# Gated linear attention followed by dropless mixture of experts: a new kernel with units across batches, transposed results by head pairs, routing beside the attention, and experts cut to their tokens

## The chip, the cores and the metric

One NeuronCore of one Trainium2 chip. The metric is the time of the kernel on the device in microseconds (us), median of several executions. All arithmetic is fp32, and each fp32 matrix product appears in the trace as two TensorE instructions.

## The reference

```python
# q, k, v, a_re, a_im: (B=4, H=8, S=768, D=48);  w1: (E=8, 384, 1024), w2: (8, 1024, 384)
mag = sqrt(a_re**2 + a_im**2);  z = (a_re + 1j*a_im) * minimum(mag, .999) / (mag + 1e-6)
for t in range(S):                       # per batch and head, state (D x D), complex
    state = z[t][:, None] * state + outer(k[t], v[t])
    y[t] = q[t] @ real(state)
x = y as (3072 tokens, H*D = 384)
logits = x @ w_gate;  e = argmax(logits);  gate_w = softmax(logits)[e]
out = gate_w * (relu(x @ w1[e]) @ w2[e])          # each token by its own expert
```

## The kernel before

The sequence is cut into chunks of 128 tokens, so there are 24 chunks, six to a batch. Two consecutive chunks of one batch form a unit (twelve units), and units follow one another batch by batch. A framework traces the program in the written order and sorts each engine's instructions itself when it builds; activations alone are held to the written order by `act` and `table`, since each change between the log/exp and the trigonometric tables is an `ACT_TABLE_LOAD` (line 135).

For a unit, `decay_steps` (lines 164 to 187) turns the gates into ln|z| and an angle on GpSimd, VectorE and ScalarE. `decay_sums` sums ln|z| over the tokens by a product with a triangular matrix (tile `csl`) and takes exp of the sum and of its negative (`E`, `Ei`). `decay_total` gets a chunk's whole decay from 16 small products with a column of ones (`ms`), whose moving operand has a single column. `angle_sums` (lines 231 to 236) sums the angles in the same way (`cst`), adds the last angle of the chunk before by a second product with `last`, and removes whole turns; `rotation` takes the sine and cosine.

`attention` (lines 283 to 315) is run per chunk. `product` (lines 251 and 255) multiplies q by `E` and k by `Ei` on GpSimd and the rotation onto both on VectorE, so a head has 96 columns. Then TensorE transposes each head of Q and K (`tp`), the transposes are copied out by ScalarE (`qt`) and VectorE (`kt`), `at` is K against Q, masked by `tri` into `am`, `dk` is K against v for the carried state `G`, and `y` is `am` against v plus `qt` against `G`. In `y` the stationary operand is `am` or `qt` (128 columns) and the moving one has the 48 columns of a head. The result is stored to `xd` in DRAM, transposed again (`tpx`, line 262) and multiplied by `w_gate` (`lp`, line 268). One `mm` helper (line 65) records all products.

Behind the attention stands a branch on the flag of gates out of range (line 370), then the routing in one piece (lines 451 to 564): argmax, gate, rank among the expert's tokens by prefix sums, and a product of one-hot matrices (`sp`) that puts the tokens into slots. Each expert has four tiles of 128 slots, whatever the number of its tokens; further tiles run under a branch at the end. For each expert `gather` (line 577) fetches its rows by indirect DMA, `turn` (line 590) transposes them to 512 columns, `expert` computes `hps` (24 products of 512 columns), then four tiles of `yps` (8 products of 384 columns each), scales by the gate and scatters the rows to the output (line 612). The weights are loaded two experts ahead (lines 106 and 108), the first two during the attention.

Of the kernel before, what the change touches and what calls it, by code (L numbers as in the profile page):

```python
# [22 lines left out]
L_MIN = -0.5  # the chunked form keeps exp(-128 * L_MIN) within fp32  # L23
# [10 lines left out]
def kernel(  # L34
# [19 lines left out]
    NT = N // P  # token tiles  # L54
    CB = S // P  # chunks of a batch
    U = 2  # chunks of a unit
    NU = NT // U
    W = U * DM
    CT = 4  # token tiles that each expert has in the static part
    NS = E * CT  # its slots, in tiles  # L60
    NR = (N - CT * P) // P  # no routing needs more tiles than that beyond them
    NB = NS + NR

# [3 lines left out]
    def copy(i, o, in_):  # L67
        (nc.scalar.copy if i % 2 else nc.vector.tensor_copy)(out=o, in_=in_)  # L68
# [4 lines left out]
    wp = ctx.enter_context(tc.tile_pool(name="wp", bufs=2))  # L73

    def const(shape, name, dt=FP):
        return cp.tile(shape, dt, name=name)

    ident = const([P, P], "ident")
    make_identity(nc, ident)
    tri = const([P, P], "tri")  # [s, t]: s <= t  # L80
    make_upper_triangular(nc, tri, val=1.0, diag=True)
    tri_turn = const([P, P], "tri_turn")
    nc.vector.tensor_scalar(out=tri_turn, in0=tri, scalar1=1.0 / math.pi, scalar2=None, op0=OP.mult)
    tri_x = const([P, P], "tri_x")  # s < t
    nc.vector.tensor_tensor(out=tri_x, in0=tri, in1=ident, op=OP.subtract)
    ones = const([P, P], "ones")
    nc.vector.memset(ones, 1.0)
    last = const([P, P], "last")  # [s, t]: s == 127
    nc.gpsimd.affine_select(
        out=last, in_=ones, compare_op=OP.is_ge, fill=0.0, base=1 - P, pattern=[[0, P]], channel_multiplier=1  # L90
    )
    mhalfpi = const([P, 1], "mhalfpi")
    nc.vector.memset(mhalfpi, -0.5 * math.pi)

    wg = const([P, KD, E], "wg")
    good = const([P, NU], "good")
    lg = const([P, NT, E], "lg")
    flag = const([1, 1], "flag", I32)

    xd = dr.tile([N, DM], FP, name="xd")  # the attention's result, by token  # L100

    W_T = {}

    def load_w(e):
        a = wp.tile([P, KD, F], FP, tag="w1", name="w1t")
        nc.sync.dma_start(out=a, in_=w1[e].rearrange("(i p) f -> p i f", p=P))
        b = wp.tile([P, KF, DM], FP, tag="w2", name="w2t")
        nc.sync.dma_start(out=b, in_=w2[e].rearrange("(i p) d -> p i d", p=P))
        W_T[e] = a, b

    # ---------------------------------------------------------------- attention
    log = ExitStack()
    xl = log.enter_context(tc.tile_pool(name="xl", bufs=2))
    psL = log.enter_context(tc.tile_pool(name="psL", bufs=1, space=PSUM))
    att = ExitStack()
    ld = att.enter_context(tc.tile_pool(name="ld", bufs=2))
    un = att.enter_context(tc.tile_pool(name="un", bufs=2))
    ch = att.enter_context(tc.tile_pool(name="ch", bufs=2))
    psM = att.enter_context(tc.tile_pool(name="psM", bufs=1, space=PSUM))
    psT = att.enter_context(tc.tile_pool(name="psT", bufs=3, space=PSUM))  # L120
    psA = att.enter_context(tc.tile_pool(name="psA", bufs=1, space=PSUM))
    psY = att.enter_context(tc.tile_pool(name="psY", bufs=1, space=PSUM))
    psD = att.enter_context(tc.tile_pool(name="psD", bufs=1, space=PSUM))
# [16 lines left out]
    def load(u, names):  # L140
        for nm, src in names:
            t = ld.tile([P, U, H, D], FP, tag=nm, name=nm)
            for c in range(U):
                b, s = divmod(u * U + c, CB)
                nc.sync.dma_start(out=t[:, c], in_=src[b, :, s * P : (s + 1) * P, :].rearrange("h t d -> t h d"))
            T[nm, u] = t.rearrange("p c h d -> p (c h d)")

    def load_a(u):
        load(u, (("ar", a_re), ("ai", a_im)))

    def load_qkv(u):
        load(u, (("q", q), ("k", k), ("v", v)))

    def decay_steps(u):
        """ln |z| and the half angle of z, z = a * min(|a|, .999) / (|a| + 1e-6)."""
        ar, ai = T["ar", u], T["ai", u]
        A = un.tile([P, W], FP, tag="A", name="A")
        L = un.tile([P, W], FP, tag="L", name="L")
        R = un.tile([P, W], FP, tag="R", name="R")
        LL = un.tile([P, U * H, 2, D], FP, tag="LL", name="LL")  # twice, for decay_total  # L160
        T["L", u], T["th", u] = LL, ai

        def s0():
            nc.gpsimd.tensor_tensor(out=A, in0=ar, in1=ar, op=OP.mult)
            nc.gpsimd.tensor_tensor(out=R, in0=ai, in1=ai, op=OP.mult)  # L165
            nc.vector.scalar_tensor_tensor(out=A, in0=A, scalar=2.0**-62, in1=R, op0=OP.max, op1=OP.add)
            act(out=L, in_=A, func=AF.Ln)

        def s1():
            act(out=R, in_=L, func=AF.Exp, scale=-0.5)  # L170
            nc.gpsimd.tensor_tensor(out=A, in0=A, in1=R, op=OP.mult)
            nc.vector.scalar_tensor_tensor(out=A, in0=ar, scalar=2.0**-62, in1=A, op0=OP.max, op1=OP.add)

        def s2():
            act(out=R, in_=R, func=AF.Ln, scale=1e-6, bias=1.0)
            nc.vector.tensor_scalar(out=L, in0=L, scalar1=0.5, scalar2=LN_CAP, op0=OP.mult, op1=OP.min)
            nc.vector.tensor_tensor(out=L, in0=L, in1=R, op=OP.subtract)

        def s3():
            act(out=A, in_=A, func=AF.Ln)  # L180

        def s4():
            act(out=A, in_=A, func=AF.Exp, scale=-1.0)
            nc.gpsimd.tensor_tensor(out=ai, in0=ai, in1=A, op=OP.mult)
            nc.vector.scalar_tensor_tensor(out=R, in0=L, scalar=-L_MIN, in1=ar, op0=OP.add, op1=OP.min)
            nc.vector.tensor_reduce(out=good[:, u : u + 1], in_=R, op=OP.min, axis=AX_X)
            nc.vector.tensor_scalar(  # L187
                out=LL, in0=bc(L.rearrange("p (x d) -> p x d", d=D), 2, 2), scalar1=L_MIN, scalar2=None, op0=OP.max
            )

        return [s0, s1, s2, s3, s4]

    def decay_angle(u):
        act(out=T["th", u], in_=T["th", u], func=AF.Arctan)

    def decay_sums(u, c):
        L = T["L", u]
        sl = slice(c * DM, (c + 1) * DM)
        if c == 0:
            T["E", u] = un.tile([P, W], FP, tag="E", name="E")  # L200
            T["Ei", u] = un.tile([P, W], FP, tag="Ei", name="Ei")
        cs = psM.tile([P, DM], FP, tag="mm", padded_shape=[P, 512], name="csl")
        mm(cs, tri, L[:, c * H : (c + 1) * H, 0])
        act(out=T["E", u][:, sl], in_=cs, func=AF.Exp)
        act(out=T["Ei", u][:, sl], in_=cs, func=AF.Exp, scale=-1.0)

    def decay_total(u):
        """exp of the chunks' sums of ln |z|, by [(re, im) d, head]."""
        ms = psM.tile([P, U, H], FP, tag="mm", padded_shape=[P, 32, 16], name="ms")
        L = T["L", u].rearrange("p x a d -> p x (a d)")  # L210
        for c in range(U):
            for h in range(H):
                mm(ms[0:DD, c, h : h + 1], L[:, c * H + h], ones[:, 0:1])
        M = un.tile([P, U, H], FP, tag="M", name="M")
        act(out=M[0:DD], in_=ms[0:DD], func=AF.Exp)
        T["M", u] = M

    def angle_sums(u, c):
        """The angle up to each token in turns, less the whole ones; on from the chunk before."""
        g = u * U + c  # L220
        if c == 0:
            T["fg", u] = un.tile([P, U * H, 2, D], FP, tag="fg", name="fg")
        hs = slice(c * H, (c + 1) * H)
        f = T["fg", u][:, hs, 1, :]
        first = g % CB == 0
        cs = psM.tile([P, H, D], FP, tag="mm", padded_shape=[P, 8, 64], name="cst")
# [452 lines left out]
```

## Time and profile before

| | |
|---|---|
| median of 3 runs | 862.42 us (859.28 to 866.72) |
| span of the profiled execution, first to last instruction | 852.1 us |
| median less that span | 10.3 us |
| TensorE busy in the span | 744.4 us (87%) |
| VectorE, GpSimd, ScalarE busy | 333.0, 224.4, 204.7 us |
| granted TensorE clock, mean over the span | 0.870 |

A busy TensorE isn't TensorE at its peak: products overlap, and the granted clock is either full (1.00, 2.4 GHz) or half (0.50, 1.2 GHz); a value between is a mean over a stretch that holds both.

### The profile page before, as it was taken

The page shows a single profiled execution, that of the slowest core. Times are in us where ns is not written, and L with a number is a line of the kernel's source. Part 1 is how long each engine was busy: PE and PEld are TensorE (multiplying, and loading weights), DVE is VectorE, ACT ScalarE, POOL GpSimd, SP SyncE. Part 2 cuts the span into 40 slices and gives each one's busy share as a digit, 9 for nine tenths or more (in the row PEclk, how much of TensorE's full clock was granted, in tenths as well). Part 3 has the DMA queues.
Part 4 walks back from the last instruction along what each step waited for, and adds up shares of the span by engine and source line. Part 5 has one row for each costly group of instructions (what it writes and reads, how often), then busy time and mean ns, then how long its engine had stood idle before and what let it go on. Part 6 is the DMA issues. An engine that isn't in the chain of part 4 may idle for free. (4 is left out here: it accounts for less than half of the span.)

```text
span 852.1 us, 8900 instructions
## 1 busy us (share of the span) xinstructions
PE 744.4 (87%) x3574; PEld 532.0 (62%) x3574; DVE 333.0 (39%) x499; ACT 204.7 (24%) x320; POOL 224.4 (26%) x177
## 2 busy tenths in 40 slices
PE   0589998999899898999991489999999999999995
PEld 0378886887878788888880435555555555555553
DVE  3577665655576376663426311111111111020200
ACT  4354244433444245533310000000000000000000
POOL 5551432616245053342000140202020303010101
PEclk9999777856897598986785679999999999999998
DMA  9475534323254232401000032324232323220000
GB/s 171 68 214 138 145 71 96 62 56 65 48 94 83 47 65 47 93 11 28 19 19 4 13 99 92 119 83 132 83 130 84 130 84 128 84 95 10 15 10 21
DMA packets 144322, 65.18 MB, mean 76 GB/s; under 512 B 127232, under 2 KB 138528, under 8 KB 144272
## 3 DMA queue, kind: packets, MB, share of 16 engines
q1 hardware_dynamic: 136720, 48.78, 25.0%
q0 software_dynamic: 4096, 11.02, 3.9%
q10 hardware_dynamic: 3456, 4.72, 1.5%
q8 instruction: 31, 0.51, 0.3%
q14 instruction: 19, 0.16, 0.1%
HBM read 55.06 MB, written 11.01 MB: 78 GB/s over the span
## 5 line engine op out<-in xcount | busy, mean ns | idle before, releaser
L65 PE MATMUL hps<-xt,w1t 128*128 128x512 f32 x384 | 168.0, 597 | 0.0
L65 PE MATMUL yps<-w2t,ht 128*128 128x384 f32 x512 | 166.4, 486 | 0.0
L65 PEld LDWEIGHTS yps<-w2t,ht 128*128 128x128 f32 x512 | 97.3, 190 | 69.5 <-issue 3.8
L65 PEld LDWEIGHTS hps<-xt,w1t 128*128 128x128 f32 x384 | 73.2, 192 | 89.1 <-issue 89.1
L612 POOL DMA_INDIRECT out_dram<-y,row x32 | 31.8, 995 | 285.1 <-DVE y L611 285.1
L611 DVE TENSOR_SCALAR y<-yps,gate 128x384 f32<-128x384 f32 x32 | 19.8, 618 | 165.4 <-PE yps L65 165.4
L65 PE MATMUL y<-v,am 128*128 128x48 f32 x384 | 75.5, 292 | 1.9 <-DVE am L291 1.8
L605 DVE TENSOR_SCALAR ht<-hps 128x512 f32<-128x512 f32 x32 | 22.1, 692 | 123.9 <-PE hps L65 123.9
L65 PEld LDWEIGHTS y<-v,am 128*128 128x128 f32 x384 | 65.2, 215 | 8.4 <-DVE am L291 3.2
L65 PE MATMUL y<-G,qt 96*128 96x48 f32 x320 | 69.5, 302 | 0.0
L65 PE MATMUL at<-qt,kt 96*128 96x128 f32 x384 | 65.2, 317 | 4.5 <-DVE am L291 4.3
L65 PEld LDWEIGHTS at<-qt,kt 96*128 96x128 f32 x384 | 58.8, 227 | 12.1 <-issue 8.1
L603 ACT ACTIVATE ht<-hps 128x512 f32<-128x512 f32 x32 | 19.1, 597 | 156.5 <-PE hps L65 133.9
L65 PEld LDWEIGHTS y<-G,qt 96*128 96x128 f32 x320 | 56.4, 220 | 0.0
L283 PE MATMUL tp<-ident,Q 128*96 128x128 f32 x192 | 41.0, 338 | 14.2 <-DVE Q L255 14.2
L251 POOL TENSOR_TENSOR Qe<-q,E 128x384 f32<-128x384 f32 x24 | 38.6, 1609 | 41.8 <-ACT E L129 40.0
L68 ACT COPY xt<-tp 128x512 f32<-128x512 f32 x8 | 4.7, 587 | 185.0 <-PE tp L590 185.0
L65 PE MATMUL csl<-LL,tri 128*128 128x384 f32 x48 | 26.1, 634 | 25.2 <-DVE LL L187 17.6
L165 POOL TENSOR_TENSOR R<-ai 128x768 f32<-128x768 f32 x12 | 18.1, 1512 | 109.6 <-DMA ai<-in_a_im_dram 109.6
L65 PE MATMUL ms<-ones,LL 128*96 128x1 f32 x384 | 42.0, 243 | 3.3 <-ACT Ei L129 3.3
L65 PEld LDWEIGHTS ms<-ones,LL 128*96 128x96 f32 x384 | 41.8, 196 | 4.4 <-ACT Ei L129 4.4
L283 PE MATMUL tp<-ident,K 128*96 128x128 f32 x192 | 41.6, 341 | 2.9 <-DVE K L255 2.9
(139 smaller groups left out, 987.8 us busy)
## 6 DMA issues: line engine op xcount, KB each, us to landing
w1t<-in_moe_w_dram SPq DMA_DIRECT2D x8, 1536.0 KB, 6.4
w2t<-in_moe_w_dram SPq DMA_DIRECT2D x8, 1536.0 KB
ar<-in_a_re_dram SPq DMA_DIRECT2D x24, 192.0 KB, 4.3
ai<-in_a_im_dram SPq DMA_DIRECT2D x24, 192.0 KB, 3.4
q<-in_q_dram SPq DMA_DIRECT2D x24, 192.0 KB, 3.8
k<-in_k_dram SPq DMA_DIRECT2D x24, 192.0 KB, 4.3
v<-in_v_dram SPq DMA_DIRECT2D x24, 192.0 KB, 3.9
xd<-x ACTq DMA_DIRECT2D x24, 192.0 KB, 1.9
```

What stands on the lines that cost most here:

```text
L65: return nc.tensor.matmul(o, lhsT=lhsT, rhs=rhs, start=start, stop=stop, skip_group_check=True)
L68: (nc.scalar.copy if i % 2 else nc.vector.tensor_copy)(out=o, in_=in_)
L165: nc.gpsimd.tensor_tensor(out=R, in0=ai, in1=ai, op=OP.mult)
L251: nc.gpsimd.tensor_tensor(out=e.rearrange("p h d -> p (h d)"), in0=T[src, u][:, sl], in1=T[dec, u][:, sl], op=OP.mult)
L283: nc.tensor.transpose(out=tp[0:DD, j], in_=X[:, hg * 4 + j], identity=ident)
L603: nc.scalar.activation(out=ht[:, f], in_=ps, func=AF.Relu)
L605: nc.vector.tensor_scalar(out=ht[:, f], in0=ps, scalar1=0.0, scalar2=None, op0=OP.max)
L611: nc.vector.tensor_scalar(out=y, in0=ps, scalar1=gates[i], scalar2=None, op0=OP.mult)
L612: nc.gpsimd.indirect_dma_start(out=out, out_offset=bass.IndirectOffsetOnAxis(ap=idx[i], axis=0), in_=y, in_offset=None, bounds_check=N - 1 ...
```

## The change

The kernel is written anew around the same mathematics.

- A unit is now one chunk position of all four batches (six units of four chunks), and it is handled in two halves of two batches. So four independent states are carried (`G0` to `G3`), and a chunk needs the one before it in its batch only four chunks later.
- The gate formula is shorter (three steps, `gate_steps`), with fixed bounds `A_MIN` and `T_MAX` in place of exact limits. Whether the gates lie within them is tested by `in_range` beside the experts. GpSimd's products move to VectorE; GpSimd keeps only DMAs.
- `ms` and the products with `last` are gone. The decay of a chunk is row 127 of `E`, stored to DRAM and read back by head dimension (`md`, `M`); the last angle goes through DRAM (`cd`) and is added to row 0 of the next unit's angles by an accumulating DMA.
- `results` computes the transposed result: v or `G` (48 columns) is stationary and `am` or `qt` (128 columns) moves. The two heads of a pair go to rows 0 and 64 of one PSUM tile `yt`. `finish` turns it back with one product per pair against `back`, which holds the identity and `w_gate` side by side, so that the logits come with it; `tpx` and `lp` are gone.
- All four `qt`/`kt` copies are ScalarE's.
- Routing runs in groups while the attention goes on (units 0 and 1, 2 and 3, 4), and only the last unit's share follows the attention. Experts are sorted by their number of tokens; place i has `CAPS[i]` columns. The expert of the first place is fixed, and its weights loaded, in the last unit.
- `hps` and the transposes have `CAPS[i]` columns; a last tile of at most 64 rows uses two or four column groups of TensorE, whose sums are added afterwards.
- Both fallbacks stand in one branch at the end.

```diff
+CAPS = (448, 416, 416, 408, 400, 384, 376, 360)
...
+        def s0():
+            act(out=A, in_=ar, func=AF.Relu, bias=a_low)
+            act(out=A, in_=A, func=AF.Ln, bias=a_min)
+            act(out=R, in_=A, func=AF.Exp, scale=-1.0)
+            tt(out=ai, in0=ai, in1=R, op=OP.mult)
+            ts(out=ai, in0=ai, scalar1=-T_MAX, scalar2=T_MAX, op0=OP.max, op1=OP.min)
+            act(out=R, in_=ai, func=AF.Square)
+        def s1():
+            act(out=R, in_=R, func=AF.Ln, bias=1.0)
+            stt(out=A, in0=R, scalar=0.5, in1=A, op0=OP.mult, op1=OP.add)
+        def s2():
+            act(out=R, in_=A, func=AF.Exp, scale=-1.0, bias=ln_eps)
+            stt(out=ar, in0=A, scalar=LN_CAP, in1=R, op0=OP.min, op1=OP.subtract)
...
+    def decay(u, half):
...
+        nc.sync.dma_start(out=md[g : g + HB, :].unsqueeze(0), in_=T["E", u, half][P - 1 : P])
+        for i in range(2):
+            nc.sync.dma_start(
+                out=M[i * D : (i + 1) * D, u, half * HB : (half + 1) * HB],
+                in_=md[g : g + HB, :].rearrange("o (h d) -> d o h", d=D),
             )
...
+    def angle(u, b0, b1):
+        th = flat(T["ai", u][:, b0:b1])
+        act(out=th, in_=th, func=AF.Arctan)
+        if u > 0:
+            nc.gpsimd.dma_start(
+                out=T["ai", u][0:1, b0:b1].rearrange("p b h d -> p (b h d)"),
+                in_=cd[1, u - 1 : u, b0 * DM : b1 * DM],
+                accum_op=OP.add,
             )
...
+    def results(u, b, hg):
+        half, c = divmod(b, HB)
+        V = T["v", u, half][:, c]
+        for hp in range(2 * hg, 2 * hg + 2):
+            o = [yt[i * 64 : i * 64 + D, hp] for i in range(2)]
+            for i in range(2):
+                mm(o[i], V[:, 2 * hp + i], T["am", u, b, hg][:, 2 * (hp % 2) + i], True, u == 0)
+            for i in range(2):
+                if u > 0:
+                    mm(o[i], T["G", b][0:DD, 2 * hp + i], T["qt", u, b, hg][0:DD, 2 * (hp % 2) + i], False, True)
...
+    def finish(u, b):
+
+        xb = psX.tile([P, HP, DD + E], FP, tag="xb", padded_shape=[P, 4, P], name="xb")
+        for hp in range(HP):
+            mm(xb[:, hp], T["ys", u, b][:, hp], back[:, hp])
...
+    for g in range(NT):
+        u, b = divmod(g, B)
...
+        at(results, g, 0)
+        at(state, g)
+        part(g, 0)
+        at(products, g + 2)
+        at(results, g, 1)
+        part(g, 1)
+        at(scores, g + 1, 0)
+        at(evict, g)
+        part(g, 2)
+        at(scores, g + 1, 1)
+        at(outer, g + 1)
+        part(g, 3)
+        at(finish, g)
...
+            if n > 64:
+                for f in range(KF):
+                    mm(ps[0:n], hs[:, f], wb[:, f], f == 0, f == KF - 1)
+                ts(out=y[0:n], in0=ps[0:n], scalar1=g, scalar2=None, op0=OP.mult)
+            else:
+
+                w = 32 if n <= 32 else 64
+                np_ = P // w
+                for f in range(KF):
+                    j = f % np_
+                    mm(ps[j * w : j * w + n], hs[:, f], wb[:, f], f < np_, f >= KF - np_)
...
+    for i in range(E):
+        turn(i)
+        if i + 1 < E:
+            gather(i + 1)
+        expert(i)
+        if i + 2 < E:
+            load_w(i + 2)
+        if i < NR_:
+            in_range(i)
```

`part` starts the gate work of the next unit at fixed quarters of a chunk. `in_range` loads a sixth of `a_re` and `a_im` (1536 columns each) and runs two VectorE operations over it.

## Rows read from the trace of the kernel before

**Rows 1.** Busy time of each engine, granted clock and DMA by stage (windows view).

```profile
0.00:47.12 47.12, 14.77 (x44) 8.38 (x45) 20.26 (x25) 19.42 (x24) 24.84 (x23) 1.00 0.88 128
47.12:447.83 400.71, 372.69 (x2484) 332.25 (x2484) 239.71 (x329) 159.78 (x255) 135.87 (x82) 0.79 0.32 72
447.83:496.65 48.82, 14.26 (x67) 11.87 (x67) 21.39 (x67) 2.23 (x3) 8.72 (x16) 0.57 0.11 30
496.65:842.39 345.74, 342.65 (x981) 179.51 (x980) 51.01 (x79) 23.22 (x39) 53.94 (x55) 0.99 0.25 83
842.39:852.10 9.71, 0.00 (x0) 0.00 (x0) 0.61 (x1) 0.00 (x0) 0.98 (x1) 0.64 0.02 5
```

Columns: stretch, its length, busy us of PE, PEld, DVE, ACT and POOL, granted clock, DMA share, GB/s.

**Rows 2.** Timeline of TensorE in the attention, at full clock (start, busy us, what).

```profile
86.60 0.88 PE L65 MATMUL csl<-LL,tri 128*128 128x384 f32 x2
87.32 0.60 PE L283 MATMUL tp<-ident,Q 128*96 128x128 f32 x4
...
89.40 0.39 PE L65 MATMUL y<-v,am 128*128 128x48 f32 x2
...
89.85 0.60 PE L283 MATMUL tp<-ident,K 128*96 128x128 f32 x4
90.29 1.48 PE L65 MATMUL dk<-v,K 128*96 128x48 f32 x16
91.60 0.51 PE L262 MATMUL tpx<-ident,x 128*128 128x128 f32 x3
91.95 1.06 PE L65 MATMUL at<-qt,kt 96*128 96x128 f32 x8
92.84 0.73 PE L65 MATMUL lp<-wg,xt 128*128 128x8 f32 x6
93.43 2.86 PE L65 MATMUL ms<-ones,LL 128*96 128x1 f32 x32
```

**Rows 3.** Windows of 2 us around two falls of the clock (columns as before).

```profile
98.00:100.00 2.00, 2.00 (x10) 1.70 (x9) 1.44 (x3) 0.00 (x0) 0.00 (x0) 0.50 0.64 86
...
146.00:148.00 2.00, 0.20 (x2) 0.14 (x2) 1.32 (x3) 1.98 (x4) 0.00 (x0) 1.00 1.15 269
...
150.00:152.00 2.00, 2.00 (x12) 1.94 (x11) 1.56 (x3) 0.61 (x2) 1.88 (x2) 0.50 0.03 5
```

**Rows 4.** Groups by line and shape: VectorE and ScalarE (busy us, mean ns).

```profile
L135 ACT ACT_TABLE_LOAD x26 | 33.4, 1283 | 1.2 <-PEq L665 0.8
L291 DVE TENSOR_TENSOR am<-at,tri 128x512 f32<-128x512 f32 x48 | 32.9, 686 | 21.6 <-PE at L65 21.5
...
L68 ACT COPY qt<-tp 96x512 f32<-96x512 f32 x48 | 27.7, 582 | 37.5 <-PE tp L283 37.2
...
L129 ACT ACTIVATE A<-A 128x768 f32<-128x768 f32 x24 | 20.3, 845 | 13.8 <-DVE A L172 13.6
...
L232 DVE TENSOR_TENSOR fg<-cst,r 128x384 f32<-128x384 f32 x24 | 13.2, 550 | 0.3
```

**Rows 5.** Timeline of TensorE in the start: its first product.

```profile
17.61 1.62 PE L65 MATMUL csl<-LL,tri 128*128 128x384 f32 x2 [17.61 <-DVE LL L187]
```

**Rows 6.** Timeline between attention and experts: end of the branch, token list.

```profile
453.77 0.14 POOL L451 IOTA eid<- 128x8 f32 x1 [54.77 <-SPq L370]
...
484.59 0.19 DVE L560 CAST tok<-sl 128x52 int32<-128x52 f32 x1
```

**Rows 7.** Timeline of TensorE over one expert.

```profile
541.70 20.77 PE L65 MATMUL hps<-xt,w1t 128*128 128x512 f32 x48
562.30 20.80 PE L65 MATMUL yps<-w2t,ht 128*128 128x384 f32 x64
582.94 1.04 PE L590 MATMUL tp<-ident,xg 128*128 128x128 f32 x8
```

**Rows 8.** DMA issues: engine, count, size, median us to landing.

```profile
w1t<-in_moe_w_dram SPq DMA_DIRECT2D x8, 1536.0 KB, 6.4
...
xd<-x ACTq DMA_DIRECT2D x24, 192.0 KB, 1.9
```

More of the change, by code (lines that the diff above doesn't have):

```diff
@@ L138, in table @@
         T["act"] = ins
[L140 to L161, printed above, removed]
-        def s0():
[L164 to L167, printed above, removed]
+    HB = B // 2
@@ new lines, with keys @@
+    owner = const([P, E], "owner", I32)
+    own0 = const([P, 1], "own0", I32)
+    tok = const([P, E, CT], "tok", I32)
+    row = const([P, E, CT], "row", I32)
+    gate = const([P, E, CT], "gate")
+    over = const([P, 1], "over")
+    head = const([P, E], "head")
+    caps = const([P, E], "caps")
+    for i, c in enumerate(CAPS):
+        nc.gpsimd.memset(caps[:, i : i + 1], float(c))
+    def keys(o):
+        cp_ = psD.tile([P, E], FP, tag="dk", padded_shape=[P, 512], name="cnt")
+        mm(cp_, ones, acc)
+        stt(out=o, in0=cp_, scalar=float(E), in1=rev, op0=OP.mult, op1=OP.add)
+        return cp_
@@ new lines, in gate_pieces, with p @@
+    def gate_pieces(n):
+        st = gate_steps(n, 0, B)
+        def p(f, *a):
+            return lambda: f(*a)
+        return {
+            -5: [p(table, "natural_log_exp_and_others"), st[0]],
+            -3: [st[1]],
+            -1: [st[2]],
+            1: [p(decay, n, 0)],
+            2: [p(decay, n, 1)],
+            3: [lambda: T["second"]() if n - 1 in GROUPS else None],
+            4: [p(table, "trig_and_small"), p(angle, n, 0, B)],
+            6: [p(turns, n, 0)],
+            7: [p(rotation, n, 0)],
+            9: [p(turns, n, 1)],
+            10: [p(rotation, n, 1)],
+        }
@@ L332 @@
+    GROUPS = {2: (0, 2), 4: (2, 4)}
+    load_gates(0, 0)
+    load_qkv(0, 0)
+    load_gates(0, 1)
+    load_qkv(0, 1)
+    for hp in range(HP):
+        for i in range(2):
+            nc.sync.dma_start(
+                out=back[i * 64 : i * 64 + D, hp, DD:], in_=w_gate[hp * DD + i * D : hp * DD + (i + 1) * D, :]
+            )
+    for half in range(2):
+        load_gates(1, half)
+    for half in range(2):
+        c0, c1 = half * HB, (half + 1) * HB
         table("natural_log_exp_and_others")
-        for f in steps:
+        for f in gate_steps(0, c0, c1):
@@ L355 @@
-    att.close()
-    bad = xl.tile([P, NU], FP, tag="bad", name="bad")
-    nc.vector.tensor_scalar(out=bad, in0=good, scalar1=0.0, scalar2=None, op0=OP.is_ge)
-    nc.vector.tensor_scalar(out=bad, in0=bad, scalar1=-1.0, scalar2=1.0, op0=OP.mult, op1=OP.add)
-    bp = psL.tile([1, NU], FP, tag="mm", padded_shape=[1, 512], name="bp")
+        angle(0, c0, c1)
+        turns(0, half)
+        rotation(0, half)
+    pieces = {1: gate_pieces(1)}
+    for i in sorted(pieces[1]):
+        if i < 0:
+            for f in pieces[1].pop(i):
+                f()
@@ new lines, in part, with at @@
+    def part(g, i):
+        for n in range(1, NU):
+            s = g * 4 + i - (n - 1) * B * 4
+            if s >= -5 and n not in pieces:
+                pieces[n] = gate_pieces(n)
+            if n in pieces:
+                for f in pieces[n].pop(s, []):
+                    f()
+    def at(f, g, *a):
+        if g < NT:
+            f(*divmod(g, B), *a)
+    at(products, 0)
+    at(products, 1)
+    at(scores, 0, 0)
+    at(scores, 0, 1)
+    at(outer, 0)
+    for g in range(NT):
+        u, b = divmod(g, B)
+        if b % HB == 0 and u + 1 < NU:
+            load_qkv(u + 1, b // HB)
+        if b in (1, 2) and u + 2 < NU:
+            load_gates(u + 2, b - 1)
+        if b == 0 and u in GROUPS:
+            T["second"] = route(*GROUPS[u])
+        if u == NU - 1 and b == 1:
+            T["second"] = route(NU - 2, NU - 1)
+            table("natural_log_exp_and_others")
+            T["second"]()
+            first_place()
+        at(results, g, 0)
[11 more added lines that the diff above has]
+        at(finish, g)
@@ new lines, with pool2, gather @@
+    T["second"] = route(NU - 1, NU)
+    places()
+    T["second"]()
+    gates_of_places()
+    att.close()
+    ex = ExitStack()
+    def pool2(name, bufs, **kw):
+        return ex.enter_context(tc.tile_pool(name=name, bufs=bufs, **kw))
+    wp = pool2("wp", 1)
+    xp = pool2("xp", 2)
+    hp = pool2("hp", 2)
+    yp = pool2("yp", 3)
+    rp = pool2("rp", 2)
+    psG = pool2("psG", 2, space=PSUM)
+    psH = pool2("psH", 4, space=PSUM)
+    psO = pool2("psO", 2, space=PSUM)
+    def gather(i):
+        xg = xp.tile([P, CT, DM], FP, tag="xg", name="xg")
+        for t in range(-(-CAPS[i] // P)):
+            n = min(P, CAPS[i] - t * P)
+            nc.gpsimd.indirect_dma_start(
+                out=xg[0:n, t],
+                out_offset=None,
+                in_=xd[:, :],
+                in_offset=bass.IndirectOffsetOnAxis(ap=tok[0:n, i, t : t + 1], axis=0),
+                bounds_check=N - 1,
+                oob_is_err=False,
+            )
+        T["xg", i] = xg
@@ new lines, in turn @@
+    def turn(i):
+        cap, xg = CAPS[i], T["xg", i]
+        xt = xp.tile([P, KD, CAPS[0]], FP, tag="xt", name="xt")
+        for d in range(KD):
+            tp = psG.tile([P, 512], FP, tag="tp", name="tp")
+            for t in range(-(-cap // P)):
+                n = min(P, cap - t * P)
+                nc.tensor.transpose(
+                    out=tp[:, t * P : t * P + n], in_=xg[0:n, t, d * P : (d + 1) * P], identity=ident[0:n, 0:n]
+                )
+            (nc.scalar.copy if d % 2 else nc.vector.tensor_copy)(out=xt[:, d, 0:cap], in_=tp[:, 0:cap])
+        T["xt", i] = xt
@@ L596, in expert @@
[L596 to L602 removed]
+                out=xg, out_offset=None, in_=xd[:, :], in_offset=bass.IndirectOffsetOnAxis(ap=ti, axis=0)
+            )
+            tp = psZ.tile([P, KD, P], FP, tag="mm", padded_shape=[P, 4, P], name="tpx")
```

870 lines of the change are left out of this document (497 added, 373 removed).

## The prediction

> **What bounds the kernel now.** I read the windows by stage first, since the page's mean over the span mixes four stages [rows 1]. Look there at TensorE's busy time against the length, and at the clock. The start (47.1 us) is bound by DMA and by the gate chain: TensorE has 14.8 us of work. In the attention (400.7 us) TensorE is busy 93%, VectorE 60%, ScalarE 40%, so TensorE sets the pace, but at a mean clock of 0.79. In the gap between attention and experts (48.8 us) nothing but routing runs. In the experts (345.7 us) TensorE is busy 99% at a clock of 0.99; only fewer columns can shorten that. The end (9.7 us) is the last scaling, scatter and drain.
>
> Next the timeline of TensorE, read by the starts of successive groups, since busy times overlap: 0.72 us for a `csl` pair, 0.112 each for `y` (0.45 for four), 0.11 for a transpose, 1.31 for 16 `dk`, 0.35 for three `tpx`, 0.111 each for `at`, 0.59 for six `lp`, 2.86 for 32 `ms` [rows 2]. `y` with 48 moving columns costs as much as `at` with 128: both have 128 stationary columns. Per chunk at full clock: 16 transposes 1.76, 16 `at` 1.78, `dk` 1.31 x 20/24 = 1.09, `y` 29.3 x 0.112 = 3.29, `tpx` 0.35, `lp` 0.59, `csl` 0.72, `cst` 0.72, `last` 0.60, `ms` 1.43; together 12.3 us. A chunk takes 400.7 / 24 = 16.7, a ratio of 0.74. The missing quarter is the clock and 7% idle time.
>
> Why the clock falls is seen in windows of 2 us. Of its 17 falls between 60 and 442 us ten come during or within 4 us of an `ms` burst, as the one to 0.50 at 98 us behind the burst of 93.43 [rows 2, 3]; most of the others follow a gap of TensorE, as that behind 146 to 148 us, where TensorE was busy 0.20 of 2 us [rows 3].
>
> **The start.** The first `csl` begins at 17.6 us [rows 5]; before, a whole second set of gates then shares the engines until the first chunk at 47.1 [rows 1]. Now half a unit goes through alone. From 17.6 I add the chain: `csl` pair at half clock 1.6, `E` and `Ei` 1.7, arctan and table 2.1, `cst` 1.6, five VectorE operations 2.7, two sines 1.7, products 1.5: about 30 us. The second half follows on the same ordered activations and unit 1's gates behind it, while chunks 0 and 1 last only some 25 us. I take 36; bounds 28 and 47.
>
> **TensorE in the attention.** `ms`, `last`, `tpx` and `lp` go: 2.97 us. Transposes, `at`, `dk`, `csl` and `cst` stay: 6.07. `results` has as many products as `y`, now with 48 stationary and 128 moving columns. No row shows that; the nearest is a transpose, 96 stationary and 128 moving at 0.11 [rows 2], so 29.3 x 0.111 = 3.26, nothing gained. `finish` adds eight products with 128 stationary and 104 moving columns, 0.89; routing's products about 0.2. Sum 10.4 us, against 12.3. The two heads of a pair write different rows of PSUM. Every row runs products one behind the other, so I take no overlap; an overlap in pairs would make `results` 1.6. The Trainium skill (TensorE: Matmul & The Clock Gate, Part 3) says that products in different column groups of the array run together; by that the sum would be 8.8 and the time that of the first rival. Against the change speaks the skill's TensorEngine Tiling (Array Packing), Key Properties: changing the tiling mode drains TensorE. No run here shows it. A group of four transposes is busy 0.60 us but starts its successor after 0.44 [rows 2], so an estimate is 0.16 lost per change, four changes a chunk, 16 us in all; by the rule 689 us, without it my sum.
>
> **VectorE and ScalarE.** Their work rises towards TensorE's. VectorE: 550 ns for 384 columns and 686 for 512 [rows 4] give 1.06 ns a column, so 0.96 for 768 and 1.77 for 1536. Per chunk: products 2 x 0.55 + 2 x 0.96 = 3.0 (half of it came from GpSimd), masks 1.37, states 0.8, turns 1.6, gates 4 x 1.77 / 4 = 1.8, small ones 0.3: 8.9. The routing of before took 21.4 us of VectorE for 24 chunks [rows 1], 0.9 per chunk: 9.8. ScalarE: 582 ns for 512 and 845 for 768 columns [rows 4], so 1.64 for 1536: copies and eviction 5 x 0.58, `x` 0.45, `E` and `Ei` 0.85, sines 0.85, seven gate functions 7 x 1.64 / 4 = 2.9, two table loads of 1.28 per unit 0.64: 8.6. So VectorE's 9.8 is the floor if TensorE got cheaper, and 10.4 TensorE's own.
>
> What waits behind what: the gate operations are now 1.6 to 1.8 us long, and a `qt` copy that comes behind one holds `at`; there are only two `tp` buffers and one `at`. `yt` is a single bank, so the results of a chunk wait for the eviction of the one before; `scores` of the next chunk stands between them in the written order and hides that. If it doesn't, each chunk pays the 0.58.
>
> **Time per chunk.** With the ratio of before, 0.74, 10.4 would become 14.1. `ms` stood before ten of seventeen falls, so I expect a clock nearer 0.88 than 0.79; TensorE's waits on the two fuller engines take back about 6%. Ratio 0.83: 12.5 us, 24 x 12.5 = 300 us. Bounds: 10.5 (no losses) and 15.5 (more waits than before), so 252 to 372.
>
> **Transfers.** `M` takes a store and two loads on SP's queue per half unit, the carry a store, a load, a VectorE operation, a store and a GpSimd accumulation. A store lands after 1.9 us, a weight load of 1.5 MB after 6.4 [rows 8]. None shows 4-byte pieces; bounds 2 and 6 each, I take 4 as for a short load, so a chain is 8 to 16 us. `M` is wanted about a unit later (50 us), the carry two thirds of a unit later: hidden, at nothing. Behind the waiting stores on SP's queue stand the q, k, v and gate loads and the stores of `x`; three buffers of halves cover them. The accumulation must land between `angle` and `turns`, some 6 us; if it's late, TensorE waits up to 5 us in each of five units, 25 us in all. The start moves 128 GB/s at a share of 0.88 [rows 1]; 28 MB in 300 us are 94 GB/s, about two thirds of that.
>
> **Gap.** The branch, 5.3 us up to 453.77, leaves this place [rows 6]; at the end one stands already. From there to the token list were 31 us [rows 6]. Now four chunks remain: one-hot matrices of 24 chunks (four operations, some 8 us) shrink to a sixth, 48 `sp` products (8.8) to eight, the tables of prefix sums go, the sorting by places comes. I count some 45 VectorE operations of 0.2 and four returns through TensorE: 14 us. From the list to the first `hps` stay 12.1 [rows 1, 6]. Together 26; bounds 18 and 36. The other groups of the routing now lie beside the attention and are in VectorE's 0.9.
>
> **Experts.** `hps` takes 20.60 us for 512 columns, four tiles of `yps` 20.64 (5.16 each) [rows 7]; an expert takes 345.74 / 8 = 43.2 [rows 1], so `turn` 1.96. The caps sum to 3208. `hps` 20.60 x 3208 / 512 = 129.1, `turn` 12.3. Tiles: 24 full ones 123.8, five short ones of 16 to 64 rows at 5.16 if nothing overlaps, 25.8; with full overlap 7.7. I take the first, as the rows run one after another: 291, bounds 273 and 295. The reference's inputs give 421 to 338 tokens per expert, all under their caps, and smallest `a_re` 0.85 above `A_MIN`, so the branch for other inputs isn't taken. `in_range` adds 12 VectorE operations of about 1.8 us, beside a VectorE busy 51 of 346 us, and 9.4 MB of loads beside 83 GB/s [rows 1]: nothing. Extra work of short tiles sits on ScalarE and VectorE too, and the last three places have none.
>
> **Sum.** 36 + 300 + 26 + 291 + 9.7 = 663 us of span instead of 852.1. The median stands 10.3 above the span of the profiled run, so 673. A measurement of this kernel can tell about 1% from no change.
>
> **Rivals.** First, the pairs overlap: TensorE's chunk 8.8, VectorE's 9.8 becomes the bound, some 11.3 us with waits, 271; experts 273. 36 + 271 + 26 + 273 + 20 = 626. For it: different PSUM rows; against: no row has two products at once. Second, the queues jam: copies and masks behind long gate operations, 15.5 us a chunk, 745. For it: three engines between 8.6 and 10.4; against: GpSimd no longer sits in the chain. Third, the experts wait: weights of place i+2 and the `in_range` loads can start only when expert i frees its buffers, 2 x 6.4 us for weights [rows 8] and some 6.6 for the check; if VectorE's check stands ahead of the next expert's copies, up to 13 us of these 19 are left in each of five places, 65 in all: 738. For it: one SP queue; against: the framework sorts instructions by what is ready. Fourth, on the other side: TensorE, now waiting on two other engines, stays at half clock through the attention, as it did behind the gap at 146 us [rows 3]. A chunk is then 10.4 / 0.5 = 20.8 and 5% idle, 21.8: 24 x 21.8 = 523, the time 896. It decides from 20.4 us a chunk, a mean clock under 0.54. Against: in the attention of before the clock came back each time, and the weakest stretches (`ms`) go.
>
> **Chances.** Forecast (640 to 705) 0.42, overlap 0.27, jam 0.15, waiting experts 0.08, half clock 0.05, near the old time by a mix of these 0.03. Range 615 to 755: it leaves out the lower end of the overlap (about 0.08), the upper end of the jam and the half clock. Faster by over 1% 0.93, within 1% 0.02, slower 0.05.
>
> **What the profile will show.** TensorE's starts of `results`: 0.11 apart or half of it. A clock near 0.88 between the first transposes and the last eviction, and 12.5 us between evictions of `yt`. First `hps` 26 us behind the last logits. 2.06 us less `hps` for each 51 columns. Wrong I would be most of all through the time per chunk: 1 us there is 24 us of the result.

## The result and the profile after

The changed kernel takes 669.57 us (median of 4 runs, 667.11 to 675.5), the kernel before 860.85 (4 runs): a ratio of 0.781, 95% interval 0.775 to 0.787. I had predicted 673. The profiled execution is the longest of the four: a span of 673.7 us and a time of 675.5; in each of the four the time is the span plus 1.8. In one kernel further down two of six executions took over 1.5% more than its fastest, and its median leaves them out.

The windows of the changed kernel by stage, to be laid beside [rows 1] (same columns):

```profile
0.00:30.13 30.13, 5.83 (x9) 2.39 (x9) 11.61 (x28) 13.90 (x15) 3.39 (x30) 1.00 1.12 172
30.13:356.88 326.75, 269.75 (x2126) 222.74 (x2126) 192.03 (x381) 179.73 (x245) 4.16 (x5) 0.85 0.42 82
356.88:382.55 25.67, 7.42 (x27) 5.12 (x27) 9.81 (x66) 0.76 (x2) 8.09 (x8) 0.51 0.70 253
382.55:663.74 281.19, 277.28 (x926) 156.93 (x925) 70.30 (x113) 25.66 (x52) 53.05 (x49) 0.99 0.36 124
663.74:673.70 9.96, 0.11 (x2) 0.00 (x0) 0.92 (x4) 0.00 (x0) 1.03 (x1) 0.72 0.09 21
```

Against the forecast: start 30.1 (36), attention 326.7 (300), gap 25.7 (26), experts 281.2 (291), end 10.0 (9.7), around the span 1.8 (10.3). The differences are -5.9, +26.7, -0.3, -9.8, +0.3 and -8.5; their sum is +2.5. That sum leads to the profiled run's 675.5; against the median, 669.6, I was 3.4 too high. The number came out right by luck: the largest error was covered by three others.

The largest one is the attention. TensorE, bound there before at 93%, is now busy 83% of it. The starts of the eviction of `yt`, read off ScalarE's timeline, tell where the rest went. Inside a unit they mostly lie 6 to 11 us apart; the five turns from a unit's last chunk to the next one's first take 42.6, 26.7, 23.5, 25.1 and 21.5.

One turn, on ScalarE's timeline of the changed kernel. The lines left out are copies and further activations of the same chain; `L149` and `L155` are the activations and table loads that the kernel chains in a fixed order:

```profile
217.26 0.83 ACT L149 ACTIVATE CS<-fg 128x768 f32<-128x768 f32 x1
218.11 1.28 ACT L155 ACT_TABLE_LOAD   x1
...
223.29 1.49 ACT L149 ACTIVATE R<-A 128x1536 f32<-128x1536 f32 x1
229.32 1.49 ACT L149 ACTIVATE R<-ai 128x1536 f32<-128x1536 f32 x1 [1.18 <-DVE ai L194]
...
235.26 1.58 ACT L149 ACTIVATE R<-A,ln_eps 128x1536 f32<-128x1536 f32 x1 [1.17 <-DVE A L199]
240.28 0.81 ACT L149 ACTIVATE E<-csl 128x768 f32<-128x768 f32 x1 [0.93 <-PE csl L64]
...
246.27 1.48 ACT L149 ACTIVATE ai<-ai 128x1536 f32<-128x1536 f32 x1
260.40 0.93 ACT L149 ACTIVATE CS<-fg,mhalfpi 128x768 f32<-128x768 f32 x1 [1.50 <-DVE fg L246]
...
270.75 0.83 ACT L149 ACTIVATE CS<-fg 128x768 f32<-128x768 f32 x1
271.60 1.28 ACT L155 ACT_TABLE_LOAD   x1
```

The next unit's gates cannot begin before the last sine of this one (217.26, then 270.75), so this is a loop of 53.5 us, and its own work (activations and table loads, copies not counted) is only some 20 us of it. From the arctan (246.27) to the first sine 14.1 us pass. What stands between is on TensorE's and GpSimd's timelines:

```profile
254.72 2.81 PE L64 MATMUL cst<-ai,tri_turn 128*128 128x384 f32 x4
...
259.83 1.56 PE L64 MATMUL cst<-ai,tri_turn 128*128 128x384 f32 x4 [1.49 <-DVE fg L244]
264.45 0.64 PE L287 MATMUL tp<-ident,K 128*96 128x128 f32 x4 [3.07 <-DVE K L278]
...
248.04 0.77 POOL L228 DMA_DIRECT2D ai<-cd  x1 [49.34 <-ACT ai L149]
```

The accumulating transfer starts at 248.04, `cst` waits for it and then for its place on TensorE, VectorE makes `fg`, and only then come the sines, the products and the transposes on which the next chunk waits. Taken from one log-table load to the next (52.26, 114.38, 168.60, 218.11, 271.60, 330.10), five loops took 277.8 us, 55.6 each: 85% of the attention.

There is a smaller loss at the same place. The copy that evicts the first chunk's `yt` stands behind the next unit's gates on ScalarE:

```profile
253.11 0.58 ACT L332 COPY ys<-yt 128x512 f32<-128x512 f32 x1 [4.50 <-PE yt L64]
...
274.84 1.58 ACT L149 ACTIVATE A<-A,a_min 128x1536 f32<-128x1536 f32 x1
...
276.79 1.49 ACT L149 ACTIVATE R<-A 128x1536 f32<-128x1536 f32 x1
278.17 0.57 ACT L332 COPY ys<-yt 128x512 f32<-128x512 f32 x1
```

The last product into that `yt` ended at 273.61, so the copy came 4.56 us late; in the turns into units 1 to 4 it was 4.25, 4.60, 4.24 and 4.56, and 0.07 in the fifth, where no gates follow. That is the jam of my second rival, in a small part. How much of it TensorE lost, no run separates.

In the experts, TensorE's timeline over places 0, 1 and 5 (caps 448, 416, 384), beside [rows 7]:

```profile
382.55 19.44 PE L64 MATMUL hps<-xt,wa 128*128 128x448 f32 x48
401.83 18.37 PE L64 MATMUL yps<-wb,ht 128*128 128x384 f32 x64
420.13 1.37 PE L635 MATMUL tp<-ident,xg 128*128 128x128 f32 x8
...
424.52 18.72 PE L64 MATMUL hps<-xt,wa 128*128 128x416 f32 x48 [1.70 <-DVE xt L638]
443.08 17.07 PE L64 MATMUL yps<-wb,ht 128*128 128x384 f32 x64
460.08 2.13 PE L635 MATMUL tp<-ident,xg 128*128 128x128 f32 x12
...
583.87 15.64 PE L64 MATMUL yps<-wb,ht 128*128 128x384 f32 x48
599.35 0.81 PE L635 MATMUL tp<-ident,xg 128*128 128x128 f32 x6
```

Three full tiles take 599.35 - 583.87 = 15.48, 5.16 each as before. With a tile of 64 rows behind them it is 18.30, so that tile costs 2.82; with one of 32 rows 17.00, so 1.52.

### The profile page after: what moved, and what is told of

The parts are those of the page before. It is cut to its first block, busy times and chain, and to the rows that moved or that the text cites. A ratio compares the mean times of both kernels' runs of the same rounds, so it can differ in the third digit from the quotient of the medians.

```text
span 673.7 us, 7954 instructions
## 1 busy us (share of the span) xinstructions
PE 560.4 (83%) x3085; PEld 387.2 (57%) x3085; DVE 284.7 (42%) x591; ACT 220.1 (33%) x313; POOL 69.7 (10%) x93
## 4 chain that ended last, share of the span: by engine, by line
PE 71%; DVE 11%; ACT 8%; DMA 6%; issue 2%; POOL 0%; SPq 0%; ACTq 0%; POOLq 0%; DVEq 0%
PE hps L64 20%; PE yps L64 18%; PE tp L287 6%; PE at L64 6%; PE yt L64 5%; PE dk L64 4%; PE cst L64 4%; PE csl L64 3%; PE xb L64 2%; DMA xd<-x 2%; ACT R L149 2%; PE tp L635 2%; DVE fg L244 1%; DMA rc<-in_a_im_dram 1%; DVE fg L243 1%
## 5 line engine op out<-in xcount | busy, mean ns | idle before, releaser
L64 PE MATMUL hps<-xt,wa 128*128 128x416 f32 (+6 forms) x384 | 134.0, 510 | 1.7 <-DVE xt L638 1.7
L64 PE MATMUL yps<-wb,ht 128*128 128x384 f32 (+6 forms) x464 | 133.6, 487 | 0.0
L64 PEld LDWEIGHTS yps<-wb,ht 128*128 128x128 f32 (+6 forms) x464 | 75.2, 175 | 56.9 <-issue 9.0
L64 PEld LDWEIGHTS hps<-xt,wa 128*128 128x128 f32 x384 | 73.5, 193 | 57.7 <-issue 31.8
L670 ACT ACTIVATE ht<-hps 128x416 f32<-128x416 f32 (+6 forms) x32 | 16.1, 504 | 126.0 <-PE hps L64 109.2
L295 DVE TENSOR_TENSOR am<-at,tri 128x512 f32<-128x512 f32 x48 | 33.0, 688 | 32.0 <-PE at L64 31.7
L64 PE MATMUL yt<-am,v 128*48 128x128 f32 x384 | 42.8, 297 | 2.9 <-DVE am L295 2.8
L617 POOL DMA_INDIRECT xg<-xd,tok x29 | 30.1, 1040 | 84.2 <-DVE bad L732 67.1
L64 PE MATMUL dk<-v,K 128*96 128x48 f32 x320 | 37.0, 270 | 1.9 <-DVE G L324 0.6
L64 PEld LDWEIGHTS dk<-v,K 128*96 128x96 f32 x320 | 36.1, 190 | 3.3 <-DVE G L326 0.9
L64 PE MATMUL csl<-ar,tri 128*128 128x384 f32 x48 | 22.2, 592 | 15.8 <-DVE ar L203 14.0
L64 PE MATMUL yt<-qt,G 96*48 96x128 f32 x320 | 34.9, 284 | 0.0
L64 PE MATMUL xb<-back,ys 128*128 128x104 f32 x192 | 30.3, 301 | 5.3 <-ACT ys L332 5.3
(145 smaller groups left out, 643.4 us busy)
```

The lines of the kernel that those rows point to most:

```text
L64: return nc.tensor.matmul(o, lhsT=lhsT, rhs=rhs, start=start, stop=stop, skip_group_check=True)
L295: tt(out=am, in0=at, in1=bc(tri, 1, 4), op=OP.mult)
L617: nc.gpsimd.indirect_dma_start(out=xg[0:n, t], out_offset=None, in_=xd[:, :], in_offset=bass.IndirectOffsetOnAxis(ap=tok[0:n, i, t : t + 1 ...
L670: nc.scalar.activation(out=ht[:, f, 0:cap], in_=ps[:, 0:cap], func=AF.Relu)
```

## The experiments

My theory (A) was that the gate chain sets the turns. Against it stood the clock (B: at half clock the chain is slow, and that is the cause), and the carry by transfers (C). All differences from the changed kernel are of medians.

**Gates once.** For units 1 to 5 `gate_steps` returns one operation:

```diff
+        if u > 0:
+            return [lambda: ts(out=ar, in0=ar, scalar1=0.1, scalar2=-0.19, op0=OP.mult, op1=OP.add)] + [lambda: None] * 2
```

> Units 1 to 5 leave out the gate chain (seven ScalarE functions less the arctan, three VectorE operations): the logarithm of the magnitude is replaced by one VectorE operation on a_re, the angle is arctan of a_im alone, so the numbers that follow are not the reference's; the check of the caps at the end is left out too. Theory A (the gate chain of the next unit is a loop as long as a unit, and the five turns from one unit to the next, which now take 21 to 43 us between two evictions of yt, wait for it): the turns fall to 9 to 14 us, the attention from 326.7 to 240 to 270 us, the time to 585 to 615. Theory B (half clock at the turns is the cause, not the result): turns stay above 20 us, the time above 645. Theory C (the carry through DRAM and its accumulating transfer): the turns stay near what they are, the time 650 to 670.

595.6 us (ratio to before 0.691, 0.686 to 0.695): 74.0 less. The turns are 12.6, 9.3, 6.8, 5.6 and 9.2 us. The mean clock of the run is 0.961 (0.90 in the profiled run of the changed kernel) with nothing done for it, so B falls as the cause: the clock rose when the waits went. (While it is low it does lengthen the loop a little: a `cst` group (x4) takes 2.81 us at 254.72 above, 1.46 at full clock in the kernel two units ahead, below.) This run takes out work as well as waits; the kernel two units ahead keeps the work.

**Earlier pieces.** All steps of `gate_pieces` but the routing's four lower, bounded in unit 1, and `load_gates` one chunk earlier:

```diff
+                n_s = s - EARLY
...
+    EARLY = 4
...
-        if b in (1, 2) and u + 2 < NU:
-            load_gates(u + 2, b - 1)
+        if b in (0, 1) and u + 2 < NU:
+            load_gates(u + 2, b)
```

> The whole computation; all pieces of a unit's gates are written one chunk (four steps) earlier, and the gate loads one chunk earlier with them. Theory A: each of the five turns gets up to one chunk of about 8.5 us shorter unless ScalarE's own order holds it back: 625 to 650. Theory B and C: the chain is as long as before and only begins earlier within the same loop; clock and carry cost the same: 660 to 680.

659.8 (659.2 to 661.2): 9.8 less, where A as I had put it foresaw 20 to 45. The shift left most of the loop. From a unit's first eviction to the next unit's (units 1 to 4) it takes 46.8, 48.5 and 48.2 us, in the changed kernel 54.2, 49.5 and 53.5, and the first turn grew from 42.6 to 54.0. Whether the 9.8 comes from the shift stays open: the framework sorts all instructions anew with every edit, and the kernel with the same rows (below), which only adds work to TensorE, came out 9.3 lower as well.

**No carry.** `if False:` before the stores in `turns` and the transfer in `angle`.

> The carry of the angle from unit to unit is left out (stores, load, VectorE operation, second store and the accumulating transfer), so the angles of units 1 to 5 start at zero and the output is not the reference's; the check of the caps at the end is left out. Theory A: only the landing of the accumulation (2 to 3 us, 8 in the first unit) leaves the chain: 645 to 665. Theory C: the carry is most of what the turns lose (97 us in all): 570 to 620. My prediction had the carry hidden, at most 25 us: 645 to 670.

641.5 (638.2 to 643.4): 28.1 less, between what A and C had foreseen. The loops, from log table to log table, are 48.1 us instead of 55.6. The carry is a part of the loop, not its whole.

**Same rows.** In `results`:

```diff
-            o = [yt[i * 64 : i * 64 + D, hp] for i in range(2)]
+            o = [yt[0:D, hp]] * 2
```

> Both heads of a pair write the same rows of PSUM (the odd head over the even one, so half of the heads are left out of x; the check of the caps is left out too), same count and shape of products. If pairs run together because they lie in different columns of the array, the starts of results go from 0.055 to 0.11 us, 1.6 us a chunk more, 39 us in all if TensorE set the pace everywhere: 700 to 710. If the chain of the gates sets the turns (theory A), only the chunks inside a unit pay, or none: 670 to 695. If the starts stay at 0.055, the pairs do not run together for that reason: 665 to 675.

660.3 (656.4 to 661.3). The starts did go to twice the distance. TensorE's timeline of the changed kernel, then of this one, four products a line, to be read as [rows 2]:

```profile
352.59 0.39 PE L64 MATMUL yt<-qt,G 96*48 96x128 f32 x4
352.81 0.39 PE L64 MATMUL yt<-am,v 128*48 128x128 f32 x4
353.03 0.39 PE L64 MATMUL yt<-qt,G 96*48 96x128 f32 x4
```

```profile
342.52 0.60 PE L64 MATMUL yt<-qt,G 96*48 96x128 f32 x4
342.96 0.60 PE L64 MATMUL yt<-am,v 128*48 128x128 f32 x4
343.40 0.60 PE L64 MATMUL yt<-qt,G 96*48 96x128 f32 x4
```

0.22 us for four against 0.44: 0.055 and 0.11 each, so the two heads of a pair do run together, and as named: when their rows of PSUM differ. (The edit also puts both heads at the same addresses. Those alone are not it: in the changed kernel the group at 352.81 goes to the next pair's addresses in the same rows, and it starts 0.22 behind the one before like the others.) Yet the time did not rise. Inside units 1 to 3 the evictions now lie 7.5 to 16.8 us apart and the turns behind them are about 14, but from a unit's first eviction to the next unit's it is 50.4, 50.4 and 51.5 us, about as before: while the loop sets the pace, that gain is worth nothing.

**Two units ahead.** If A is right, the loop must break when no sine waits in ScalarE's order for what follows its own arctan:

```diff
+        m = n + 1
...
-            4: [p(table, "trig_and_small"), p(angle, n, 0, B)],
-            6: [p(turns, n, 0)],
-            7: [p(rotation, n, 0)],
-            9: [p(turns, n, 1)],
-            10: [p(rotation, n, 1)],
+            4: [p(table, "trig_and_small"), p(rotation, n, 0)],
+            5: [p(rotation, n, 1)],
+            6: [p(angle, m, 0, B), p(carry, m, 0, B)] if m < NU else [],
```

Here `m` is the unit whose gates and arctan are made, one further ahead; `turns(n)` go to steps -5 and -3, the transfer becomes a function `carry` behind the arctan, unit 1's gates go into the start, and `load_gates` fetches unit u + 3.

> The whole computation. The gates and the arctan of unit n+1 are done in the same two phases of ScalarE's fixed order as the sums and the sines of unit n, so that no sine waits in that order for the carry, cst and the VectorE operations between it and the arctan; unit 1's gates move into the start. Theory A, made sharper (the loop is ScalarE's fixed order of activations: 53.5 us from the sines of one unit's second half to those of the next, of which 14.1 lie between arctan and the first sine and 9.5 between the two pairs of sines): the loop falls to some 33 us, under the 41 us that four chunks take without the gate chain, so TensorE sets the pace again: turns of 9 to 14 us, the first half unit's followers some 12 us later, in all 595 to 625. Theory B (clock): 655 to 675. Theory C (the carry's own time, wherever it stands): as without the carry at best, 640 to 650.

633.4 (632.6 to 634.9; ratio to before 0.736, 0.733 to 0.740): 36.2 less, 5.4% under the changed kernel, with the whole computation. Its windows over the first units and the rest:

```profile
30.00:142.70 112.70, 68.42 (x468) 54.67 (x469) 62.93 (x93) 68.39 (x78) 1.88 (x2) 0.74 0.54 92
142.70:315.90 173.20, 170.62 (x1653) 148.45 (x1651) 130.15 (x289) 111.26 (x166) 2.27 (x3) 1.00 0.46 92
```

From chunk 4's eviction (142.7) on TensorE is busy 99% at full clock, the turns are 9.8, 9.1, 9.2 and 8.0 us, and 19 chunks take 173.2: 9.1 each. ScalarE's loops (log-table loads at 155.45, 190.68, 234.70, 271.36) are 35 to 44 us and hold up no chunk any more. That shows A, with all of the work kept; the late copies of the first chunks are gone as well (0.04 to 0.42 us). But chunk 4 comes 56.0 us behind chunk 3, and so I missed 595 to 625. The evictions of chunks 3, 4, 15 and 16:

```profile
86.75 0.59 ACT L334 COPY ys<-yt 128x512 f32<-128x512 f32 x1 [0.54 <-PE yt L64]
...
142.74 0.59 ACT L334 COPY ys<-yt 128x512 f32<-128x512 f32 x1
...
246.25 0.59 ACT L334 COPY ys<-yt 128x512 f32<-128x512 f32 x1 [1.43 <-PE yt L64]
...
255.46 0.59 ACT L334 COPY ys<-yt 128x512 f32<-128x512 f32 x1 [1.43 <-PE yt L64]
```

Why chunk 4 is late is on the same kernel's timelines of SyncE, GpSimd and TensorE:

```profile
65.18 0.50 SPq L252 DMA_DIRECT2D cd<-fg  x1
```

```profile
77.00 1.09 POOL L230 DMA_DIRECT2D ai<-cd  x1 [73.04 <-DMA cd<-carry]
```

```profile
83.82 1.46 PE L64 MATMUL cst<-ai,tri_turn 128*128 128x384 f32 x4
...
91.92 2.93 PE L64 MATMUL csl<-ar,tri 128*128 128x384 f32 x4 [2.10 <-DVE fg L246]
```

Unit 1's `csl` stands behind its `cst` (they share one buffer of PSUM), and that behind the carry of unit 0, whose second half was first stored at 65.18. From the table load at 67.47 until `csl`, ScalarE's chain has nothing to do; its next activation starts at 94.88. Then unit 2's gates still stand ahead of unit 1's first sine (99.44 to 114.71).

**Start filled.** So `decay(1, 0)` went into the start's first phase and unit 1's `turns` and `rotation` ahead of unit 2's gates:

```diff
+            0: [p(turns, n, 0), p(rotation, n, 0)],
+            2: [p(turns, n, 1), p(rotation, n, 1)],
+            4: [p(table, "natural_log_exp_and_others"), p(decay, n, 1), st[0]],
...
```

> The whole computation; as the kernel two units ahead, but the exponents of unit 1's first half are made in the start's first phase and unit 1's sines in the start's second phase, so that unit 1 does not wait for the gates of unit 2. With the kernel two units ahead the evictions of yt from chunk 4 on came every 9.1 us (173.2 us for 19), but chunk 4 came 56 us behind chunk 3. If the loop was the whole loss (theory A), chunk 4 now follows chunk 3 within 15 us and the rest keeps 9.1 to 9.5 us: 590 to 605. If the 27 us in which ScalarE did nothing of the chain had another reason (the carry's landing, for one), 615 to 635.

635.5 (634.5 to 636.1): no gain. Chunk 4 now follows chunk 3 after 28.8 us, but chunk 2 comes 37.0 behind chunk 1 (21.2 in the changed kernel) and chunks 4 to 11 are 8.7 to 16.2 apart, 12.2 on average (9.6 in the kernel two units ahead). The wait went from one place of the start to three.

**Start filled, same rows.** Now that TensorE sets the pace from chunk 11 on, the pairs were put on the same rows again.

> As the start-filled kernel, but both heads of a pair write the same rows of PSUM (the odd head over the even one, half of the heads left out of x; the check of the caps left out). There TensorE sets the pace, so 32 products a chunk at 0.11 instead of 0.055 us cost up to 1.6 us a chunk in some 20 chunks: 25 to 35 us more than the start-filled kernel. If VectorE or ScalarE set the pace there, under 10.

653.1 (652.2 to 655.8): 17.6 more, so the expectation was too high. From chunk 11 to 23 the evictions come every 10.6 us (209.5 to 336.2) against 9.1 (207.7 to 317.0): 1.45 a chunk, as expected, but for the second half only; chunk 11 comes just 1.8 us later, so in the first half the waits hide it. The windows, of the start-filled kernel and of this one:

```profile
199.00:319.00 120.00, 118.48 (x1151) 103.84 (x1149) 84.57 (x190) 68.61 (x109) 0.76 (x1) 1.00 0.37 85
```

```profile
199.00:338.00 139.00, 138.06 (x1151) 125.48 (x1150) 82.98 (x187) 69.09 (x107) 0.76 (x1) 1.00 0.36 77
```

**Start filled, no carry.**

> As the start-filled kernel without the carry of the angle (stores, load, VectorE operation, second store and accumulating transfer; units 1 to 5 begin at angle zero, the check of the caps is left out). Theory A: out of the loop the carry costs next to nothing, within 6 us of the start-filled kernel, except for the first unit. Theory C: 15 to 28 us less, as in the changed kernel.

631.5 (629.5 to 633.1): 4.0 less, against 28.1 in the changed kernel; the last eviction comes 8.2 us earlier (308.84, before 317.03). Out of the loop the carry costs little, so C falls as the cause of the turns. Nor is it the whole of the start's loss: without it chunk 2 comes 46.7 us behind chunk 1.

**Plain short tiles.** `if n > 64` became `if True`.

> The whole computation; the five short tiles of the experts go the way of the full ones, eight products one behind the other with all rows. If the short tiles of the changed kernel run in column groups (2.8 us for 64 rows, about 1.5 for 16 to 32 rows, against 5.16), this costs 5 x 5.16 - 2.8 - 4 x 1.5 = 17 us: 684 to 690. If their gain is taken back by the adds and copies behind them, within 5 us of 669.6.

685.4 (683.7 to 690.7): 15.8 more, near the expected 17: the adds and copies behind the column groups take little or nothing back.

**Caps of 512.** `CAPS = (512,) * 8`.

> The whole computation with every cap at 512. By columns: hps 20.60 x (4096 - 3208) / 512 = 35.7 us more, turns some 2, tiles 32 x 5.16 = 165.1 in place of 24 x 5.16 + 8.8 = 132.6, 32.5 more: 70 us in all, 735 to 745. If the experts waited for weights or the check of the range instead of TensorE, less than 50.

737.1 (733.8 to 744.1): 67.5 more, nearly the 70 of the columns. The time of the experts goes by TensorE's columns.

**No range check.** The call of `in_range` left out.

> The loads and VectorE operations that check the range of the gates beside the experts are left out (the result counts as in range). My prediction had them at nothing: 666 to 672. If they hold up the first gather and the copies of the experts, the gap falls from 25.7 to about 21 and single waits of 1 to 2 us in the experts go: 660 to 665.

670.4 (666.3 to 672.2): nothing, as predicted.

**Weights behind the gather.** On the start-filled kernel, `load_w(1)` and `load_w(2)` by `nc.gpsimd`, written behind `gather(0)`.

> As the start-filled kernel, with the weights of places 1 and 2 issued by GpSimd behind its first gathers instead of by SP ahead of them. If the weights' transfers hold up the first gather, the first hps comes 22 us behind the last logits instead of 25.7 and the time is 3 to 4 us under the start-filled kernel; if the gather's own issue and landing set it, no change.

638.8 (638.0 to 640.6): 3.3 more, and the first `hps` comes 26.6 us behind the last logits instead of 25.5. The sorted order still put the first weight ahead of the gathers, so whether the weights delay them was not settled.

## Why the prediction came out right, step by step

**Time per chunk: two steps failed, in opposite directions.** The first is "I take no overlap": `results` at 3.26 us a chunk. It runs at 0.055 us a product, 29.3 x 0.055 = 1.6 (same rows: 0.11). This was a term twice too large, and my first rival's overlap is what happens. The Trainium skill (TensorE: Matmul & The Clock Gate, Part 3) says that products in different column groups run together; the 0.055 against 0.11 agrees. Both sums I had weighed are seen once TensorE is left alone: 8.8 with overlap is 9.1 measured, 10.4 without is 10.6. The second is the step from 10.4 to 12.5 by a ratio of 0.83. I took losses as a share, from a clock and some waits, and for ScalarE I took 8.6 us of busy time per chunk and stopped there. Its work is indeed small (179.73 / 24 = 7.5 us a chunk), but its activations stand in a fixed order with waits in it, and that order closes into a loop of 55.6 us per unit, 13.9 a chunk. The attention took 13.6 a chunk instead of 12.5; with the loop open and the pairs together it takes 9.1 from chunk 4 on. Gates once, no carry and two units ahead show this loop from three sides. None of my rivals named it. The jam (745) came nearest; its late copies are there (some 4.4 us in each of four turns), but the turns take 21 to 43.

**Transfers "hidden, at nothing": failed for the carry.** I had given 25 us as its price if it came late; taking it away gained 28.1. That it costs little once out of the loop is the 4.0. `M`'s loads land after 2.4 us (I took 4), and no operation waits for them.

**VectorE's floor of 9.8** was too high: 192.03 / 24 = 8.0 us a chunk, and 9.1 a chunk were reached with VectorE busy 130.15 of 173.2 us.

**The clock** was forecast at 0.88 and came out at 0.85 in the attention. That `ms` was behind its falls is not contradicted. Now the low clock goes with TensorE's waits: 0.74 while the start's waits last and 1.00 after them, in the kernel two units ahead.

**Start.** It took 30.1, the chain alone, but two errors of mine met in that. The timeline of TensorE in the changed kernel:

```profile
14.00 2.90 PE L64 MATMUL csl<-ar,tri 128*128 128x384 f32 x4 [14.00 <-DVE ar L203]
20.66 2.92 PE L64 MATMUL cst<-ai,tri_turn 128*128 128x384 f32 x4 [3.76 <-ACT ai L149]
...
30.13 1.06 PE L287 MATMUL tp<-ident,K 128*96 128x128 f32 x4 [6.55 <-DVE K L278]
```

The first `csl` begins at 14.00 instead of 17.61 [rows 5], and from there to the first transposes it is 16.1 us where my terms add up to 12.9: `csl` and `cst` of a half unit are two products each (x4), 2.9 us, and I had taken one each, 1.6. That the second half stands behind it is true, but not ahead of the first transposes, where I had added 6.

**Gap.** 25.7, as predicted, but the parts differ: the token list (366.96, where [rows 6] has 484.59) is there after 10.1 us (14), and from it to the first `hps` are 15.6 (12.1).

**Experts.** `hps` is 132.7 summed over places (129.1; places 0 and 1 ran 1.3 and 1.8 over), tiles 132.9 instead of 149.6, because short tiles overlap (131.5 by my other bound), transposes and waits 15.6 (12.3).

**Around the span.** I set the median against one span. They belong to different executions; a run's time is its span plus 1.8.

**Mode changes.** The Trainium skill (TensorEngine Tiling (Array Packing), Key Properties) says that a change of tiling mode drains TensorE. I had estimated 0.16 us per change for this, 16 us in all (96 of them are 15.4). TensorE's timeline of the start-filled kernel has such changes, into the pairs and out of them:

```profile
115.97 1.16 PE L64 MATMUL at<-qt,kt 96*128 96x128 f32 x8
117.06 0.31 PE L64 MATMUL yt<-am,v 128*48 128x128 f32 x1
...
127.27 0.39 PE L64 MATMUL yt<-qt,G 96*48 96x128 f32 x4
127.59 0.64 PE L289 MATMUL tp<-ident,Q 128*96 128x128 f32 x4
```

Four `yt` products start 0.32 us ahead of the transposes behind them, 0.22 ahead of the next `yt`: 0.10 lost. Eight `at` start mostly 1.09 ahead of a `yt` and 0.89 to 1.00 ahead of transposes: 0.1 to 0.2. With both heads in the same rows it is as much (0.53 for 0.44, and 1.09). So some 0.1 us is lost at such a change, whether the pairs run together or not. That this is a drain, no run shows; and 9.1 measured against 8.8 leaves at most 0.3 us a chunk for all of them, about 7 in the attention.

## What to carry to other kernels

Where one engine's instructions are put in a fixed order, follow that order once around, with each wait in it, and compare its length with the time of the work that it feeds: busy time per chunk says nothing of such a loop. Before pricing a gain on the engine that was the bound, ask which loop binds after the change: the same halved products were worth nothing in the changed kernel and 17.6 us once the loop was open. Here the loop was opened by taking waits out of it (work on the unit after next in the same phase); starting its pieces earlier left most of it.

## What was not expected of the hardware

Eight products of 384 columns that are spread over two column groups and accumulate in one bank of PSUM took 2.82 us instead of 5.16, and over four 1.52: a half and a quarter of 5.16, and 0.24 and 0.23 more. TensorE's granted clock stayed at 1.00 for 173 us of products as short as 0.055 us each, in a kernel whose start had 0.74. How to fill that start (56 us between chunks 3 and 4, or the same loss spread out) stays open.
